# Float32 scores for the first 20 heads, maxima transposed in their own slot, and four constant matmuls at the head of ten slots

## The chip, the core and the metric

The kernel runs on one core of one Trainium2 chip. The metric is the device time of one execution in microseconds. TensorE (PE in the profile) multiplies matrices and PEld loads its weights, VectorE (DVE) reduces and combines, ScalarE (ACT) applies functions, GpSimd (POOL) works elementwise, and SyncE (SP) only issues DMAs. GpSimd and ScalarE issue DMAs too, each in the order of its own instructions.

## What is computed

Block-causal attention for 8 batches of 8 heads, and then a two-layer network with a gate on the joined heads:

```python
batch, n_heads, seq, head_dim = (8, 8, 576, 64)
scores = scale * np.matmul(q, k.transpose(0, 1, 3, 2))        # scale = 1/8
mask = block_i >= block_j                                      # blocks of 64
scores = np.where(mask, scores, -1000000000.0)
attn = np.exp(scores - np.max(scores, axis=-1, keepdims=True))
attn = attn / (np.sum(attn, axis=-1, keepdims=True) + 1e-09)
x = np.matmul(attn, v)                    # heads joined: 4608 x 512
h = x @ w_in                              # 512 x 2048
sp = np.maximum(h, 0.0) + np.log1p(np.exp(-np.abs(h)))
out = (h * erf(sp)) @ w_out               # 2048 x 512
```

q and k are scaled so that the scores are large; all arrays are float32.

## The kernel before

**Slots.** The 64 heads are worked through one per slot. In slot n the kernel computes the exponentials of head n's scores (`probs`, lines 437 to 468), the row maxima of head n+2 (`maxes`, lines 393 to 435), starts the load of head n+3 (`load_qk`, lines 377 to 391), and in every second slot multiplies two heads' exponentials with V (`pv`, lines 470 to 523). Every fourth slot normalises four heads and writes their part of x to DRAM (`normalise`, line 547). Beside that run the conversion of the network's weights (`conv`, two half weights in most early slots, lines 116 to 126; `split_w`, lines 141 to 148, from slot 9) and, from slot 10 on, steps of the network itself (`moe1`, line 267; up at line 190, gate at lines 159 to 167, down at line 199): none in slots 0 to 9 that find work, 12 steps a slot to slot 19, 28 from slot 20. What is left of the network follows after the last slot.

**Order.** Each slot is a set of lists of steps; each list has a stretch of the slot, for example 0 to 0.6, its steps are spread evenly over it, and `merge` (line 214) sorts all steps of the slot by that place. Each engine then works its own instructions in a fixed order and waits for what an instruction needs. Buffers are in rings; a step that writes a buffer waits for its last reader.

**Scores.** Head n has one buffer of `qks`, four heads deep (line 265), with four parts of 576 columns: klh, qhl, kh, qh. kh and qh are k and q rounded to float32r as a GpSimd DMA writes them; klh and qhl hold in one half of the partitions what rounding left off (`low`, lines 388 and 389, two subtractions on GpSimd, from an exact copy `st` that SP loads, two buffers deep) and in the other half the rounded values. A piece of the scores is two matmuls into one bank (lines 446 and 447): kh with qh, over 64 rows, four mask rows and one row with the negated maxima, and klh with qhl over 128 rows. ScalarE takes the exponential (line 451). There are six pieces with 1856 columns in all.

**Maxima.** Each step a, b, c, d(0), d(1) of `maxes` is one or two matmuls of rounded q and k (line 400) and VectorE reductions (line 403). Step e transposes the five columns of maxima on TensorE (line 430), ScalarE copies them (line 432) and issues the DMA that puts them as one row into the head's buffer (line 433; "qk<-mt" in the profile). The five steps of head n+2 are spread over slot n; e is put off to slot n+1, where it is alone in the stretch 0 to 0.6.

**Start.** Three heads are loaded; the mask rows come once from DRAM on GpSimd's queue and are copied to the other three buffers by DMAs on ScalarE's queue (lines 586 to 599). In slots 0 and 1 ten constant matmuls each (`warm`, line 646: a 128 x 32 array of ones, 512 columns, float16, into a bank that nothing reads) are spread over the slot.

**V.** In the first three batches (`B32`), V and the exponentials are kept in float32 and line 495 multiplies them in float32; later they are split into two float16 parts, three products each.

Of the kernel before, what the change touches and what calls it, by code (L numbers as in the profile page):

```python
# [32 lines left out]
def tile_attention_moe(ctx: ExitStack, tc: tile.TileContext, qk, v, w, maskrows, sels, out):  # L33
# [13 lines left out]
    T = 256  # L47
    GA = 8
    B32 = 3
    SH = 384  # L50
    N = B * H

# [209 lines left out]
    scaled = [False, False]  # L262
    todo = []
    NB = 4
    qks = [wpool.tile([P, 4 * S + 64], F32R, name=f"qk{i}", bufs=1) for i in range(NB)]

    def moe1(ready):

# [25 lines left out]
    with tc.tile_pool(name="apool", bufs=2) as apool, tc.tile_pool(name="spool", bufs=1) as spool, \  # L294
# [77 lines left out]

        def part(n, i):

            return qks[n % NB][:, i * S : (i + 1) * S]

        def load_qk(n):
            b, h = divmod(n, H)
            t = qks[n % NB][:, : 4 * S].rearrange("p (i n) -> p i n", n=S)
            st = apool.tile([P, S], F32, tag="st", name=f"st_{n}", bufs=2)  # L380

            def a():
                nc.gpsimd.dma_start(t[:D, 1:4, :], qk[b, h, D:].rearrange("(s d) n -> d s n", d=D))
                nc.sync.dma_start(st, qk[b, h, : 2 * D])
                nc.gpsimd.dma_start(t[D:, 0:2, :], qk[b, h, : 2 * D].rearrange("(s d) n -> d s n", d=D))

            def c():
                nc.gpsimd.tensor_tensor(out=t[:D, 0, :], in0=st[:D, :], in1=f32(t[:D, 2, :]), op=ALU.subtract)  # L388
                nc.gpsimd.tensor_tensor(out=t[D:, 1, :], in0=st[D:, :], in1=f32(t[D:, 1, :]), op=ALU.subtract)  # L389

            return a, c

        def maxes(n):

            mx, K = mxs[n % 2], D + 4
            kh, qh = part(n, 2), part(n, 3)

            def mm(dst, i, k0, w_):
                r = min(P, S - i * P)
                nc.tensor.matmul(dst[:r, :w_], lhsT=qh[:K, i * P : i * P + r], rhs=kh[:K, k0 : k0 + w_], start=True, stop=True)  # L400

            def red(col, src, r=P):
                nc.vector.tensor_reduce(out=mx[:r, col : col + 1], in_=src, axis=AX.X, op=ALU.max, negate=True)  # L403

            def a():
                s = bank(f"s01_{n}")
                mm(s, 0, 0, 256)
                mm(s[:, 256:], 1, 0, 256)
                red(0, s[:, :128])
                red(1, s[:, 256:])  # L410

            def b():
                s = bank(f"s2_{n}")
                mm(s, 2, 0, 384)
                red(2, s[:, :384])

            def c():
                s = bank(f"s3_{n}")
                mm(s, 3, 0, 512)
                red(3, s)  # L420

            def d(j):
                s = bank(f"s4_{n}_{j}")
                mm(s, 4, 288 * j, 288)
                red(5 + j, s[:64, :288], 64)

            def e():
                nc.vector.tensor_reduce(out=mx[:64, 4:5], in_=mx[:64, 5:7], axis=AX.X, op=ALU.min)
                pt = bank(f"mt{n}")
                nc.tensor.transpose(out=pt[:5, :P], in_=mx[:, :5], identity=ident)  # L430
                mt = apool.tile([5, P], F32R, tag="mt", name=f"mt_{n}")
                nc.scalar.copy(mt, pt[:5, :P])
                nc.scalar.dma_start(f32(qks[n % NB][D + 4 : D + 5, 3 * S :]).rearrange("o (i p) -> o i p", p=P), f32(mt))

            return [a, b, c, lambda: d(0), lambda: d(1), e]

        def probs(n, out):
# [4 lines left out]
            def one(j, q0, w_, o):  # L442
                kk = min(P, S - j * P)
                ks = slice(j * P, j * P + kk)
                s = bank(f"t{j}_{n}_{q0}")
                nc.tensor.matmul(s[:kk, :w_], lhsT=kh[:K, ks], rhs=qh[:K, q0 : q0 + w_], start=True, stop=False)  # L446
                nc.tensor.matmul(s[:kk, :w_], lhsT=klh[:, ks], rhs=qhl[:, q0 : q0 + w_], start=False, stop=True)  # L447
                skip = max(0, starts[j] - q0)
                part, c = offs[j]
                c += q0 + skip - starts[j]  # L450
                nc.scalar.activation(p32s[part][:kk, c : c + w_ - skip], s[:kk, skip:w_], AF.Exp, scale=SCALE)  # L451
# [132 lines left out]
        vs, prs, usbs = {}, {}, {}  # L584
        normals, ready_at, ready = {}, {}, 0
        heads = [load_qk(n) for n in range(NB - 1)]
        masks = [qks[n][D : D + 5, 2 * S : 4 * S] for n in range(NB)]
        nc.gpsimd.dma_start(masks[0], maskrows)
        for m in masks[1:]:
            nc.scalar.dma_start(f32(m), f32(masks[0]))  # L590
        heads[0][0]()
        sel = spool.tile([P, 4], F32, name="sel")
        nc.sync.dma_start(sel, sels)
# [30 lines left out]

        PRIO = {}
        WARM = 10
        LQ = 0.1
        TOF = {0: 1, 1: 1, 2: 2, 3: 2, 4: 2, 5: 2, 6: 2, 7: 2, 8: 2} | {n: 2 for n in range(11, 19)}
        SCALE_AT = {9: 0, 20: 1}
# [20 lines left out]
        for n in range(N + 3):  # L650
# [3 lines left out]
                lists += [(late("load", [load]), 0, LQ), (late("low", [low]), LQ, 1)]  # L654
            if n + 2 < N:
                *steps, rows[n + 2] = maxes(n + 2)
                lists.append((late("max", steps), 0, 1))
            if n + 1 in rows:
                lists.append((late("max", [rows.pop(n + 1)]), 0, 0.6))
            if n < N:  # L660
                prs[n] = []
                lists.append((late("prob", probs(n, prs[n])), 0, 1))
# [77 lines left out]
```

## Time and profile before

| | |
|---|---|
| median of 3 runs | 1251.46 us (1250.63 to 1252.27) |
| the profiled execution | 1253.77 us, span 1252.0 us |
| TensorE busy | 1169.7 us, 93% |
| ScalarE busy | 865.4 us, 69% |
| VectorE busy | 791.9 us, 63% |
| GpSimd busy | 515.9 us, 41% |
| DMA | 151.73 MB, mean 121 GB/s |
| granted TensorE clock, mean | 0.970 |

The profile gives times from the first instruction on. In a view of waits, a row names the engine and line that stood idle, what ended its wait, the total in us, how often, and the longest one. In the chain of work that ended last, and in the timeline, a row has start, duration, engine and line. The view of windows gives busy time by engine in stretches of the span, with the clock that TensorE was granted as a share of full speed. "t" is a bank of scores, "s" a bank of scores for the maxima, "u" one of products with V; "qk<-qk" is the load of a head. A matmul's recorded time includes its way through the array, so the pace of a stream is read from the starts of its matmuls. A matmul on float32 operands is recorded as two matmuls and two weight loads.

### The profile page before, as it was taken

What the parts mean: (1) busy time and instruction counts of PE and PEld (TensorE: products, weight loads), DVE (VectorE), ACT (ScalarE), POOL (GpSimd) and SP (SyncE); (2) the same over time, 40 slices, a digit from 0 to 9 for tenths busy, and PEclk for the clock granted to TensorE, in tenths of its full rate; (3) what the DMA queues carried; (4) which work ended last, traced back from release to release, by engine and by line L of the source; (5) the groups of instructions that cost most, each with busy time, mean ns of one, the idle gap of its engine ahead of it and who ended that gap; (6) DMA issues with size and microseconds to landing.
All of it is one profiled execution on the core that took longest, in us unless ns stands there. A gap on an engine that the chain in (4) does not pass through costs nothing.

```text
span 1252.0 us, 23446 instructions
## 1 busy us (share of the span) xinstructions
PE 1169.7 (93%) x9018; PEld 811.0 (65%) x9018; DVE 791.9 (63%) x1457; ACT 865.4 (69%) x1699; POOL 515.9 (41%) x486
## 2 busy tenths in 40 slices
PE   5788699989999999999999899999999999999896
PEld 2465466666666767767767677766777766666563
DVE  4677689787577666676657667666666644343433
ACT  1465577687676777877777677777777876666664
POOL 6455446545343444445444353545443313121211
PEclk9876799999999999999999999999999999999999
DMA  9988569744544455364454455455554121121211
GB/s 218 250 208 190 124 181 234 195 101 117 112 128 110 115 125 128 100 147 120 99 124 116 118 119 130 112 124 128 112 137 108 45 78 53 60 76 35 64 55 51
DMA packets 95741, 151.73 MB, mean 121 GB/s; under 512 B 7738, under 2 KB 44922, under 8 KB 95630
## 3 DMA queue, kind: packets, MB, share of 16 engines
q1 hardware_dynamic: 69840, 93.34, 25.7%
q0 software_dynamic: 25120, 56.66, 22.6%
q8 instruction: 71, 1.16, 0.4%
q10 hardware_dynamic: 670, 0.23, 0.2%
q14 instruction: 40, 0.33, 0.1%
HBM read 121.66 MB, written 28.31 MB: 120 GB/s over the span
## 4 chain that ended last, share of the span: by engine, by line
PE 49%; DVE 20%; ACT 18%; DMA 7%; issue 4%; POOL 1%; DVEq 0%; SPq 0%; POOLq 0%; ACTq 0%
PE m_h L190 16%; PE o L199 15%; PE u L495 5%; DVE m_r L163 4%; DVE m_r L164 4%; DVE m_r L165 3%; ACT m_r L160 3%; ACT m_r L162 3%; ACT m_r L161 3%; ACT m_r L159 3%; PE t L446 3%; PE s L400 3%; PE t L447 2%; DMA qk<-qk 2%; DMA qk<-mt 2%
## 5 line engine op out<-in xcount | busy, mean ns | idle before, releaser
L190 PE MATMUL m_h<-xh,w 128*128 128x256 f16 x2304 | 476.1, 276 | 19.5 <-DVE m_r L165 12.2
L190 PEld LDWEIGHTS <-w 128*128 128x128 f16 x3456 | 328.3, 99 | 158.1 <-issue 31.2
L199 PE MATMUL o<-w,m_gh 128*128 128x512 f16 x1152 | 334.1, 382 | 12.2 <-DVE pt L240 4.9
L167 POOL TENSOR_TENSOR m_gl<-m_r,m_gh 128x512 f16<-128x512 f32 x144 | 171.8, 1193 | 391.1 <-ACT m_gh L166 340.6
L190 PE MATMUL m_h<-xl,w 128*128 128x256 f16 x1152 | 316.8, 275 | 0.5 <-DMA xl<-x_d 0.5
L403 DVE TENSOR_REDUCE mx<-s 64x1 f32<-64x288 f32 (+4 forms) x384 | 174.5, 469 | 131.3 <-PE s L400 130.5
L163 DVE SCALAR_TENSOR_TENSOR m_r<-m_r,m_r 128x512 f32<-128x512 f32 x144 | 112.8, 783 | 197.3 <-ACT m_r L162 190.8
L199 PE MATMUL o<-w,m_gl 128*128 128x512 f16 x576 | 203.7, 384 | 0.3 <-POOL m_gl L167 0.3
L451 ACT ACTIVATE p<-t 128x288 f32<-128x288 f32 (+4 forms) x384 | 144.6, 384 | 79.4 <-PE t L447 69.1
L166 ACT CAST m_gh<-m_r 128x512 f16<-128x512 f32 x144 | 88.9, 617 | 157.2 <-DVE m_r L165 154.4
L446 PE MATMUL t<-qk 69*128 69x288 f32 (+4 forms) x384 | 168.2, 439 | 13.0 <-DMA qk<-mt 6.8
L400 PE MATMUL s<-qk 68*64 68x288 f32 (+3 forms) x384 | 150.1, 423 | 22.8 <-DMA qk<-qk 19.8
L159 ACT ACTIVATE m_r<-m_h,c,bs 128x512 f32<-128x512 f32 (+3 forms) x192 | 124.1, 666 | 44.5 <-PE m_h L190 41.4
L388 POOL TENSOR_TENSOR qk<-st,qk 64x576 fp32r<-64x576 f32 x64 | 95.9, 1499 | 127.2 <-DMA qk<-qk 124.5
L199 PEld LDWEIGHTS <-m_gh 128*128 128x128 f16 x1152 | 100.2, 98 | 67.6 <-issue 12.3
L164 DVE SCALAR_TENSOR_TENSOR m_r<-m_r 128x512 f32<-128x512 f32 x144 | 122.6, 852 | 3.3
L447 PE MATMUL t<-qk 128*128 128x288 f32 (+4 forms) x384 | 120.0, 313 | 0.0
L463 DVE TENSOR_TENSOR p<-p,p 128x832 f16<-128x832 f32 x80 | 81.7, 1022 | 58.0 <-ACT p L462 57.9
L389 POOL TENSOR_TENSOR qk<-st,qk 64x576 fp32r<-64x576 f32 x64 | 98.4, 1538 | 39.2 <-DMA qk<-qk 29.1
L161 ACT ACTIVATE m_r<-m_r,c 128x512 f32<-128x512 f32 x144 | 103.8, 721 | 2.7 <-ACT m_r L160 0.7
L162 ACT ACTIVATE m_r<-m_r,c 128x512 f32<-128x512 f32 x144 | 103.7, 720 | 2.3 <-ACT m_r L161 0.3
L160 ACT ACTIVATE m_r<-m_r,c 128x512 f32<-128x512 f32 x144 | 103.7, 720 | 1.6
(99 smaller groups left out, 1454.8 us busy)
## 6 DMA issues: line engine op xcount, KB each, us to landing
qk<-qk POOLq DMA_DIRECT2D x64, 432.0 KB, 5.0
st<-qk SPq DMA_DIRECT2D x64, 288.0 KB
qk<-qk POOLq DMA_DIRECT2D x64, 288.0 KB, 5.6
raw<-w SPq DMA_DIRECT2D x32, 512.0 KB
v<-v SPq DMA_DIRECT2D x16, 640.0 KB
x_d<-xs POOLq DMA_DIRECT2D x32, 288.0 KB, 3.3
xh<-x_d SPq DMA_DIRECT2D x36, 256.0 KB
xl<-x_d SPq DMA_DIRECT2D x36, 256.0 KB
```

The costliest lines, as they stand in the source:

```text
L159: nc.scalar.activation(r0s[:, :, lo:hi], h[:, :, lo:hi], AF.Tanh, bias=const(p1), scale=bss[b][g][:, 0:1])
L161: nc.scalar.activation(r0, r1, AF.Square, bias=const(b2), scale=a2)
L163: nc.vector.scalar_tensor_tensor(out=r0, in0=r0, scalar=c4, in1=r1, op0=ALU.add, op1=ALU.mult)
L164: nc.vector.scalar_tensor_tensor(out=r0, in0=r0, scalar=c5, in1=r0, op0=ALU.add, op1=ALU.mult)
L167: nc.gpsimd.tensor_tensor(out=gl, in0=r0, in1=gh, op=ALU.subtract)
L190: nc.tensor.matmul(h[:, k, :], lhsT=wf[:, a, sl], rhs=x[:, cc, :], start=cc == 0 and i == 0, stop=cc == NCC - 1 and i == 2)
L199: nc.tensor.matmul(o[c], lhsT=a[:, sl], rhs=wf[:, b_, :], start=u == u0 and k == 0 and not lo and b_ == 2, stop=u == u1 - 1 and k == nu - ...
L400: nc.tensor.matmul(dst[:r, :w_], lhsT=qh[:K, i * P : i * P + r], rhs=kh[:K, k0 : k0 + w_], start=True, stop=True)
L403: nc.vector.tensor_reduce(out=mx[:r, col : col + 1], in_=src, axis=AX.X, op=ALU.max, negate=True)
L446: nc.tensor.matmul(s[:kk, :w_], lhsT=kh[:K, ks], rhs=qh[:K, q0 : q0 + w_], start=True, stop=False)
L447: nc.tensor.matmul(s[:kk, :w_], lhsT=klh[:, ks], rhs=qhl[:, q0 : q0 + w_], start=False, stop=True)
L451: nc.scalar.activation(p32s[part][:kk, c : c + w_ - skip], s[:kk, skip:w_], AF.Exp, scale=SCALE)
```

## The change

For heads 0 to 19 (`N32`) the scores are one float32 matmul per piece, with exact k and q in a float32 buffer; the maxima of these heads are still taken from rounded k and q, which now lie in a buffer of their own (`lows`). These heads are loaded by two DMAs of 288 KB, one on GpSimd's queue into `lows` and one on SP's into `qks`, and have no subtractions. From head 20 on the buffers of `qks` are taken anew as float32r and `lows` holds klh and qhl; scores and subtractions are as before, rounded values come by three DMAs in place of two with the same bytes in all, and heads 20 to 23 load the mask rows again. At the start, `lows` and `qks` both get mask rows, seven DMAs on ScalarE's queue in place of three.

In slots 0 to 9 (`SOON`), the five steps of the maxima of head n+2 are spread over 0 to 0.7, step e follows at 0.9 of the same slot, and four of the constant matmuls stand at the head of the slot (0 to 0.04). Slots 0 and 1 keep their ten as well. In slot 0 the row of head 1, put off from before the loop, is still transposed in the stretch 0 to 0.6.

```diff
+    N32 = 20
...
-    qks = [wpool.tile([P, 4 * S + 64], F32R, name=f"qk{i}", bufs=1) for i in range(NB)]
+    lows = [wpool.tile([P, 2 * S], F32R, name=f"ql{i}", bufs=1) for i in range(NB)]
+    qks = [wpool.tile([P, 2 * S + 64], F32, tag="qk", name=f"q32_{i}", bufs=NB) for i in range(NB)]
...
-            return qks[n % NB][:, i * S : (i + 1) * S]
+            return (lows if i < 2 else qks)[n % NB][:, i % 2 * S : (i % 2 + 1) * S]
...
-            t = qks[n % NB][:, : 4 * S].rearrange("p (i n) -> p i n", n=S)
+            if N32 <= n < N32 + NB:
+                qks[n % NB] = wpool.tile([P, 2 * S + 64], F32R, tag="qk", name=f"qk{n}", bufs=NB)
+            lo, hi = [x[n % NB][:, : 2 * S].rearrange("p (i n) -> p i n", n=S) for x in (lows, qks)]
+            if n < N32:
+                src = qk[b, h, : 2 * D].rearrange("(s d) n -> d s n", d=D)
+
+                def whole():
+                    nc.gpsimd.dma_start(lo[:D], src)
+                    nc.sync.dma_start(hi[:D], src)
+
+                return whole, lambda: None
...
             def a():
-                nc.gpsimd.dma_start(t[:D, 1:4, :], qk[b, h, D:].rearrange("(s d) n -> d s n", d=D))
+                if n < N32 + NB:
+                    nc.gpsimd.dma_start(qks[n % NB][D : D + 5, : 2 * S], maskrows)
+                nc.gpsimd.dma_start(hi[:D], qk[b, h, : 2 * D].rearrange("(s d) n -> d s n", d=D))
+                nc.gpsimd.dma_start(lo[:D, 1, :], qk[b, h, D : 2 * D])
                 nc.sync.dma_start(st, qk[b, h, : 2 * D])
-                nc.gpsimd.dma_start(t[D:, 0:2, :], qk[b, h, : 2 * D].rearrange("(s d) n -> d s n", d=D))
+                nc.gpsimd.dma_start(lo[D:], qk[b, h, : 2 * D].rearrange("(s d) n -> d s n", d=D))
...
-            kh, qh = part(n, 2), part(n, 3)
+            kh, qh = [part(n, i) for i in ((0, 1) if n < N32 else (2, 3))]
...
-                nc.tensor.matmul(s[:kk, :w_], lhsT=kh[:K, ks], rhs=qh[:K, q0 : q0 + w_], start=True, stop=False)
-                nc.tensor.matmul(s[:kk, :w_], lhsT=klh[:, ks], rhs=qhl[:, q0 : q0 + w_], start=False, stop=True)
+                nc.tensor.matmul(s[:kk, :w_], lhsT=kh[:K, ks], rhs=qh[:K, q0 : q0 + w_], start=True, stop=n < N32)
+                if n >= N32:
+                    nc.tensor.matmul(s[:kk, :w_], lhsT=klh[:, ks], rhs=qhl[:, q0 : q0 + w_], start=False, stop=True)
...
-        masks = [qks[n][D : D + 5, 2 * S : 4 * S] for n in range(NB)]
-        nc.gpsimd.dma_start(masks[0], maskrows)
-        for m in masks[1:]:
-            nc.scalar.dma_start(f32(m), f32(masks[0]))
+        nc.gpsimd.dma_start(lows[0][D : D + 4], maskrows[:4])
+        for n in range(NB):
+            if n:
+                nc.scalar.dma_start(f32(lows[n][D : D + 4]), f32(lows[0][D : D + 4]))
+            nc.scalar.dma_start(qks[n][D : D + 5, : 2 * S], maskrows)
...
+        SOON = 10
...
                 *steps, rows[n + 2] = maxes(n + 2)
-                lists.append((late("max", steps), 0, 1))
+                lists.append((late("max", steps), 0, 0.7 if n < SOON else 1))
             if n + 1 in rows:
                 lists.append((late("max", [rows.pop(n + 1)]), 0, 0.6))
+            if n < SOON:
+                lists.append((late("max", [rows.pop(n + 2)]), 0.8, 1))
+                lists.append(([warm] * 4, 0, 0.04))
```

More of the change, by code (lines that the diff above doesn't have):

```diff
@@ L373, in part @@
         def part(n, i):
-            return qks[n % NB][:, i * S : (i + 1) * S]
+            return (lows if i < 2 else qks)[n % NB][:, i % 2 * S : (i % 2 + 1) * S]
         def load_qk(n):
             b, h = divmod(n, H)
-            t = qks[n % NB][:, : 4 * S].rearrange("p (i n) -> p i n", n=S)
+            if N32 <= n < N32 + NB:
[7 more added lines that the diff above has]
+                return whole, lambda: None
             st = apool.tile([P, S], F32, tag="st", name=f"st_{n}", bufs=2)
             def a():
-                nc.gpsimd.dma_start(t[:D, 1:4, :], qk[b, h, D:].rearrange("(s d) n -> d s n", d=D))
+                if n < N32 + NB:
+                    nc.gpsimd.dma_start(qks[n % NB][D : D + 5, : 2 * S], maskrows)
+                nc.gpsimd.dma_start(hi[:D], qk[b, h, : 2 * D].rearrange("(s d) n -> d s n", d=D))
+                nc.gpsimd.dma_start(lo[:D, 1, :], qk[b, h, D : 2 * D])
                 nc.sync.dma_start(st, qk[b, h, : 2 * D])
-                nc.gpsimd.dma_start(t[D:, 0:2, :], qk[b, h, : 2 * D].rearrange("(s d) n -> d s n", d=D))
+                nc.gpsimd.dma_start(lo[D:], qk[b, h, : 2 * D].rearrange("(s d) n -> d s n", d=D))
             def c():
-                nc.gpsimd.tensor_tensor(out=t[:D, 0, :], in0=st[:D, :], in1=f32(t[:D, 2, :]), op=ALU.subtract)
-                nc.gpsimd.tensor_tensor(out=t[D:, 1, :], in0=st[D:, :], in1=f32(t[D:, 1, :]), op=ALU.subtract)
+                nc.gpsimd.tensor_tensor(out=lo[:D, 0, :], in0=st[:D, :], in1=f32(hi[:D, 0, :]), op=ALU.subtract)
+                nc.gpsimd.tensor_tensor(out=lo[D:, 1, :], in0=st[D:, :], in1=f32(lo[D:, 1, :]), op=ALU.subtract)
             return a, c
@@ L432, in e @@
                 nc.scalar.copy(mt, pt[:5, :P])
-                nc.scalar.dma_start(f32(qks[n % NB][D + 4 : D + 5, 3 * S :]).rearrange("o (i p) -> o i p", p=P), f32(mt))
+                nc.scalar.dma_start(f32(qks[n % NB][D + 4 : D + 5, S:]).rearrange("o (i p) -> o i p", p=P), f32(mt))
             return [a, b, c, lambda: d(0), lambda: d(1), e]
```

## The prediction

> **What bounds the kernel now.** I read the windows first, cut where the stages end: the first score matmul of a slot (line 446) gives slot 0 its start at 24.75 us, slot 10 at 118.84 and slot 20 at 255.02. The columns are busy time by engine (with a count), then granted TensorE clock, DMA share and GB/s.
>
> ```profile
> core 0: us, PE busy (x) PEld busy (x) DVE busy (x) ACT busy (x) POOL busy (x), PEclk, DMA share, GB/s
> 0.00:24.75 24.75, 11.04 (x32) 5.04 (x32) 7.45 (x21) 1.54 (x2) 17.43 (x37) 1.00 1.13 228
> 24.75:118.84 94.09, 78.00 (x484) 52.12 (x484) 68.56 (x157) 53.55 (x147) 43.22 (x41) 0.78 0.92 223
> 118.84:255.02 136.18, 120.92 (x880) 81.93 (x879) 105.24 (x207) 93.18 (x216) 69.17 (x59) 0.91 0.70 177
> 255.02:1252.00 996.98, 959.72 (x7625) 671.87 (x7625) 610.68 (x1075) 717.15 (x1336) 386.13 (x350) 0.99 0.40 101
> ```
>
> Behind slot 20 TensorE is busy for 959.72 of 996.98 us at a clock of 0.99: it is the bound there, and the instructions of heads 20 and later stay what they were. The change therefore acts on the first 255 us. In the start-up nothing but loads matters. In slots 0 to 9 three things are short together: the DMA engines are 92% taken, TensorE is idle for 16.1 us, and the clock gives away 22% of 94.09 us, 20.7 us. In slots 10 to 19 TensorE is idle for 15.3 us and the clock loses 9% of 136.18 us, 12.3 us.
>
> Next, whom TensorE waits for, first between 25 and 60 us, then 60 to 100, then 100 to 160 (us in total, times, longest):
>
> ```profile
> PE s L400 <- DMA qk<-qk: 5.0, 2, 2.7
> PE t L446 <- DMA qk<-mt: 4.7, 3, 2.9
> ```
> ```profile
> PE s L400 <- DMA qk<-qk: 2.2, 2, 1.4
> PE t L446 <- DMA qk<-mt: 2.1, 2, 1.1
> ```
> ```profile
> PE m_h L190 <- DMA xh<-x_d: 7.2, 1, 7.2
> ```
>
> Of the 16.1 idle us in slots 0 to 9, 7.2 wait for a head's load and 6.8 for the row of maxima, which travels by DMA from its transpose (line 430) to the head's buffer; half of the 15.3 later ones is one wait for the first x tile. The chain of waits shows how the start hangs together (start, us, what):
>
> ```profile
> 14.47 1.41 POOL qk L389
> 15.89 0.33 SPq L384
> 16.27 0.47 SPq L326
> 16.84 8.15 DMA raw<-w
> 25.01 0.68 ACT a L120
> ...
> 26.44 3.44 DMA qk<-mt
> ```
>
> The low part on GpSimd, SP's next head load that waits for it, the v load and the weight load queued behind that on SP, ScalarE's conversion of the weights, and behind it the row of maxima.
>
> Last, the clock in shorter stretches (same columns as above):
>
> ```profile
> 71.00:85.00 14.00, 12.37 (x46) 8.23 (x47) 9.83 (x17) 8.21 (x20) 7.58 (x6) 0.51 0.78 184
> 108.00:112.00 4.00, 4.00 (x50) 3.63 (x40) 2.96 (x10) 3.06 (x9) 1.26 (x2) 1.00 0.60 165
> 112.00:126.00 14.00, 12.77 (x52) 8.02 (x50) 12.05 (x31) 8.92 (x20) 8.79 (x6) 0.51 0.61 122
> 136.00:147.00 11.00, 6.18 (x32) 4.26 (x32) 2.13 (x3) 1.91 (x3) 2.78 (x2) 0.53 0.83 156
> ```
>
> TensorE counts as busy through most of two stretches of 14 us at half clock; one of them follows on 4 us without a gap.
>
> **The change part by part.** *Float32 scores, heads 0 to 19.* Two float32r matmuls per piece (lines 446 and 447) become one in float32. First the old price, at full clock, by starts:
>
> ```profile
> 49.72 0.31 PE L446 MATMUL t<-qk 69*128 69x320 f32 x1
> 49.88 0.31 PE L447 MATMUL t<-qk 128*128 128x320 f32 x1
> 50.02 0.63 PE L400 MATMUL s<-qk 68*128 68x256 f32 x3
> ```
>
> A pair of 320 columns takes 0.30 us, 0.93 ns a column, and a head has 288+288+256+256+448+320 = 1856 columns, 1.73 us. No float32 score exists in this trace; the nearest rows are the products with V, float32 in the first three batches and float16 later:
>
> ```profile
> 303.70 3.00 PE u L495 x28
> 308.40 0.86 PE o L199 x4
> 314.37 1.67 PE us L518 x24
> ```
> ```profile
> 375.55 2.18 PE u L495 x42
> ```
>
> Both of line 495 cover 2 x 1600 columns, the two heads of a pair in the two halves of the array. In float16 with three terms that is 9600 columns in 2.18 us, 0.23 ns each, so the halves run side by side: one matmul alone takes 0.42 ns a column (four of 512 at line 199 in 0.86 us). In float32, 1600 column pairs in 3.00 us are 1.88 ns each, four times that and a little. A float32 score fills the array alone, so a head costs between 1856 x 4 x 0.42 = 3.1 us and 1856 x 1.88 = 3.5 us; I take 3.3, 1.6 more than now. If the halves did not run side by side, the low end, a head would cost 1.7 and nothing be added. Twenty heads at 1.6: 16 us in slots 0 to 9 and 16 in slots 10 to 19, on the engine nearest to being the bound.
>
> *Loads and low parts of heads 0 to 19.* The 432 and 288 KB on GpSimd's queue and 288 KB on SP's become 288 and 288 KB. The maxima read their own buffer, whose last reader is three slots back, so its load no longer waits for the probabilities of the slot before. The two subtractions go from GpSimd, and with them SP's wait for their staging buffer. What I read of it:
>
> ```profile
> qk<-qk POOLq DMA_DIRECT2D x14, 432.0 KB, 6.4
> qk<-qk POOLq DMA_DIRECT2D x13, 288.0 KB, 6.8
> ```
> ```profile
> SPq L384 <- POOL qk L389: 34.4, 8, 8.9
> ```
>
> The first two are DMA issues of 0 to 119 us (count, KB each, us to landing), the last is SP's wait from 24 to 119. By 119 us some 14 heads save 432 KB each, 6 MB of the 223 GB/s x 119 us = 26.5 MB moved: the DMA engines then need about 92 us for what takes 119, so they stop being the bound, and the 7.2 us of waits for loads go. At the start, SP issues its v and weight loads without the wait for the subtraction: the chain loses the 1.41 us at 14.47, and the first load is 288 KB in place of 720 KB on one queue. I take 5 us off the start-up; the bounds are 1 (the subtraction alone) and 8 (the whole stretch from 16.84 to 25.0 that waits for weights).
>
> *Maxima transposed in their own slot.* Their row is issued some 0.4 slot earlier, about 4 us with slots of 9.4 (94.09/10), which is more than the longest single wait for it, 2.9: the 6.8 us go. The price is a wait that the trace hardly has: the transpose stands in TensorE's order soon after its last score, and VectorE must have reduced it. Queued behind it are the next slot's scores, and ScalarE's exponentials wait for those. The nearest row is TensorE's wait for VectorE's reductions at the scores, over the first 320 us:
>
> ```profile
> PEld t L446 <- DVE mx L403: 4.8, 7, 1.3
> ```
>
> Bounds: 0, and the 1.3 of the longest, in every slot; I take 0.2 a slot, 2 us in all, which is about what these waits come to per slot now (4.8 us over some 24 slots), because VectorE keeps a quarter of this stage free.
>
> *Four constant matmuls in each of ten slots.* Each streams 512 columns in float16, 0.215 us at full clock by line 199's row: forty cost 8.6 us, 17 at half clock, and nothing where they fall into idle time.
>
> *The clock.* At full clock the work of slots 0 to 9 now lies between 52 us, summed from rows (ten heads at 1.73 for scores and 1984 columns at half of 0.93 ns, 0.9, for maxima, four pairs at 3.00 + 1.67, two normalisations at some 3.5, of which line 556 is 1.24, below), and busy time by clock, 78.0 x 0.78 = 61. I take 57, which is 61% of 94.09 us.
>
> ```profile
> 224.83 1.24 PE rt L556 x12
> ```
>
> After the change it is 57 + 16 + 8.6 = 81.6 us in fewer microseconds, above 85%. Both half-clock stretches of 14 us ended only in the long unbroken float32 products with V:
>
> ```profile
> 81.38 4.36 PE L495 MATMUL u<-p,v 128*64 128x128 f32 x22
> ```
> ```profile
> 120.95 5.48 PE L495 MATMUL u<-p,v 128*64 128x256 f32 x28 [0.52 <-ACT p L451]
> ```
>
> Float32 scores are the same kind of stream. I take the clock to 0.95 in slots 0 to 9 and 0.97 in the next ten.
>
> The page "TensorE: Matmul & The Clock Gate" of the Trainium skill (Part 1: The HAM clock gate) has the clock halve only after a window of some 3.4 us without work and rise after as long a busy one. The rows of 71 to 85 and 108 to 126 speak against that: 4.00 busy of 4.00 us and then half clock, and 12.37 of 14 us busy without a rise. By that rule four constant matmuls are too short to lift the clock, and yet it would stay full as soon as the long waits go; what that would give is the second rival.
>
> *The sum.* Start-up: -5. Slots 0 to 9: 81.6 of work, 4 of idle time (16.1 - 7.2 - 6.8 = 2, and 2 at the transposes), 4.3 lost to the clock, 89.9 against 94.1: -4.2. Slots 10 to 19: +16 of scores, -5 of the 7.2 at the first x tile, whose load stood on SP behind a head load held up by a subtraction, -8.3 of clock (12.3 to 4), -2 of other idle time filled: +0.7. Behind slot 20, one more GpSimd issue per head, 44 at 0.65 us, and four mask loads lie in GpSimd's free time (386.13 of 996.98 us busy): 0, or some 3 if a tenth of them holds something up. Together -8.5.
>
> ```profile
> L383 POOL DMA_DIRECT2D qk<-qk x64 | 41.4, 646 | 129.0 <-PE t L447 112.1 <-PE o L199 12.6 <-PE s L400 3.7
> ```
>
> ```profile
> 123.83 9.12 SPq L384 DMA_DIRECT2D st<-qk  x2
> 133.12 0.39 SPq L222 DMA_DIRECT2D xh<-x_d  x1
> ```
>
> The last two rows are those of SP on which the -5 rests. The profiled execution took 1253.77 us (span 1252.0), the median of the runs is 1251.46; 8.5 off the median is 1243.
>
> **The rivals.** *Slower: float32 at the clock of today.* If the clock follows waiting rather than streaming and stays at 0.78 and 0.91, the added 24.6 us cost 31.5 in slots 0 to 9 on top of 78.0 busy, with 4 idle 113.5 (+19.4); slots 10 to 19 get 16/0.91 - 7 = +10.6; with -5 at the start +25, 1276. It decides from the point where less than half of the lost clock comes back (there the sum is near +8, 1260). For it: 12.77 of 14 us busy at a clock of 0.51. Against: those stretches are full of short, latency-bound matmuls.
>
> *More gain: all of the lost clock returns.* If the half clock comes only of waiting, it goes with the waits for loads, maxima and x tile: the 4.3 and the 4 left in the sum go too, 1234.5; with 8 at the start, 1231.5. This is the page's rule carried through. For it: those waits were most of TensorE's idle time. Against it: the half-clock stretches with little idle time.
>
> *No change: VectorE and ScalarE set the pace.* VectorE is busy 68.56 of 94.09 and 105.24 of 136.18 us; if the removed waits come back as waits of the transposes and exponentials (the bound of 1.3 us a slot in place of 0.2, 11 us in slots 0 to 9), the gain of 8.5 is gone: 1251 to 1254.
>
> **How the numbers follow.** Forecast 0.42, more gain 0.21, no change 0.14, slower 0.23. About 0.2%, 2.5 us, is what a measurement can tell. Below 1249 lie the larger gain and nine tenths of the forecast, with a little of the no-change case: 0.62. Within: 0.12; above: 0.26. The range goes from 1229, below the larger gain, to 1260, where half of the clock comes back; beyond it lies the worse half of the slower case.
>
> **What would show it.** Right: no wait of line 446 for the row of maxima and none of line 400 for loads before 119 us; a granted clock of 0.9 or more in slots 0 to 9; a float32 score of 288 columns every 0.48 to 0.54 us; slot 0 starting near 20 us and slot 10 near 110; the stretch behind slot 20 within 3 us of 997. Wrong: a clock still under 0.85, transposes waiting for VectorE by over 1 us a slot, slots 10 to 19 longer than 142 us, or a score at half the price assumed.

## The result, and the profile after

The changed kernel takes 1258.1 us, the median of 20 runs (1249.26 to 1268.42), the kernel before 1251.57 (20 runs): a ratio of 1.0053, 95% interval 1.0033 to 1.0073 (it leaves out the run of 1268.42 as a slow one). It is slower by half a per cent; 8.5 us faster was forecast. The profiled execution of the changed kernel took 1252.59 us, 5.5 under its own median; that of the kernel before, 1253.77, lies 2.2 over its own. So the two profiles show a difference of -1.2 us where the runs show +6.5. The runs of the changed kernel say where the rest is: at a mean granted clock of 0.982 or more they take 1249 to 1254 us (one 1262.6), at 0.975 to 0.978 they take 1257 to 1268.

To set the profiles side by side I cut both at the same instruction of each slot, the exponential of the 64 rows of a head's last block, in slots 0, 9 and 20. Windows of the kernel before (length, busy time of PE, PEld, DVE, ACT and POOL with counts, clock, DMA share, GB/s):

```profile
0.00:26.32 26.32, 12.61 (x43) 6.50 (x44) 8.79 (x24) 2.85 (x7) 17.43 (x37) 1.00 1.14 234
26.32:116.19 89.87, 73.78 (x464) 48.64 (x464) 64.57 (x151) 50.12 (x139) 41.00 (x40) 0.79 0.94 227
116.19:274.39 158.20, 140.91 (x1011) 95.55 (x1010) 126.80 (x248) 110.60 (x251) 82.69 (x69) 0.92 0.66 164
274.39:1252.00 977.61, 942.39 (x7505) 660.27 (x7503) 591.78 (x1037) 701.85 (x1307) 374.83 (x341) 0.99 0.40 101
```

And of the changed kernel:

```profile
0.00:28.20 28.20, 15.25 (x45) 6.77 (x45) 10.62 (x26) 3.36 (x7) 6.36 (x28) 1.00 0.98 199
28.20:118.30 90.10, 89.74 (x505) 48.36 (x503) 58.96 (x151) 50.90 (x138) 10.00 (x14) 0.90 0.65 183
118.30:276.38 158.08, 148.14 (x1006) 93.56 (x1007) 118.15 (x245) 110.40 (x248) 50.08 (x51) 0.95 0.53 138
276.38:1250.80 974.42, 943.72 (x7508) 661.09 (x7505) 587.53 (x1038) 703.39 (x1308) 393.82 (x381) 0.99 0.39 102
```

The second row of each is the case. The stage lasts as long as before, 90.10 against 89.87 us, but it is another stage: the DMA share went from 0.94 to 0.65, GpSimd from 41 us to 10, the clock from 0.79 to 0.90, and TensorE from 73.78 us busy to 89.74 of 90.10. TensorE's waits between the two cuts are one row:

```profile
PE s L415 <- DVE mx L418: 0.3, 1, 0.3
```

The chain of waits, summed by line over this stage, before and after (the answer breaks off at the right):

```profile
by line: DMA qk<-mt 28.4%; PE u L495 21.7%; PE t L446 8.8%; DMA qk<-qk 8.2%; PE us L518 6.4%; PE s L400 5.9%; PE t L447 5.2%; ACT p L451 2.6%; ACT a L120 1.8%; issue 1.4%; PE rb L575 1.3%; PE rt L556 1.3%; ACT mt L432 1.2%; PE mt L430 0.8%;
```
```profile
by line: PE t L461 35.5%; PE u L511 14.4%; PE s L415 13.8%; PE warm L665 12.1%; DMA v<-v 6.3%; PE us L534 5.6%; PE rb L591 3.7%; PE mt L445 1.7%; DVE vm L338 1.6%; PE rt L572 1.4%; DVE mx L418 1.1%; DVE w L148 0.7%; DVE usb L593 0.7%; issue
```

Before, 28% of the chain is the way of the maxima and 8% the loads of heads. Afterwards neither is in the row, and float32 scores (line 461, "t") and constant matmuls (line 665, "warm") have taken their room. One slot of that chain, without a gap on TensorE:

```profile
41.33 0.49 PE t L461 x2
41.82 3.00 PE u L511 x28
44.82 0.43 PE s L415
45.25 0.43 PE t L461 x2
45.68 0.13 PE s L415
45.82 0.11 PE vt L340
45.93 0.57 PE t L461 x2
46.51 0.28 PE s L415
46.78 0.75 PE t L461 x2
47.53 1.67 PE us L534 x24
49.20 0.20 PE mt L445
49.41 0.54 PE t L461 x2
49.95 0.97 PE warm L665 x4
```

With the piece of 0.49 just ahead of it (at 40.66), a head's six scores take 0.49 + 0.49 + 0.43 + 0.57 + 0.75 + 0.54 = 3.27 us; four constant matmuls take 0.97.

The half clock has not gone. It stands at the two normalisations of the stage, in slots 5 and 9; the first of the two, and the full-clock stretch behind it:

```profile
72.70:86.40 13.70, 13.70 (x41) 7.10 (x42) 7.63 (x18) 5.72 (x15) 4.62 (x5) 0.50 0.55 162
...
86.40:113.60 27.20, 27.20 (x195) 16.02 (x191) 14.38 (x40) 13.20 (x38) 1.84 (x3) 1.00 0.50 133
```

TensorE is busy for all of the 13.7 us at half clock, and constant matmuls stand in them (1.39 us for three at 75.86, in the chain).

### The profile page after: what moved, and what is told of

Read it like the earlier page. It is cut to its first block, busy times and chain, and to the rows that moved or that the text cites. A ratio compares the mean times of both kernels' runs of the same rounds, so it can differ in the third digit from the quotient of the medians.

```text
span 1250.8 us, 23571 instructions
## 1 busy us (share of the span) xinstructions
PE 1196.8 (96%) x9058; PEld 809.8 (65%) x9058; DVE 775.3 (62%) x1457; ACT 868.1 (69%) x1699; POOL 460.3 (37%) x474
## 4 chain that ended last, share of the span: by engine, by line
PE 48%; DVE 21%; ACT 20%; DMA 5%; issue 4%; POOL 1%; DVEq 0%; ACTq 0%; POOLq 0%; SPq 0%
PE m_h L191 14%; PE o L200 14%; PE t L461 5%; DVE m_r L164 5%; DVE m_r L165 4%; PE u L511 4%; DVE m_r L166 4%; ACT m_r L161 4%; ACT m_r L162 4%; ACT m_r L163 3%; PE s L415 3%; ACT m_r L160 3%; ACT m_gh L167 2%; DVE p L479 2%; DMA v<-v 2%
## 5 line engine op out<-in xcount | busy, mean ns | idle before, releaser
L200 PE MATMUL o<-w,m_gh 128*128 128x512 f16 x1152 | 336.2, 384 | 10.8 <-ACT ob L243 4.4
L160 ACT ACTIVATE m_r<-m_h,c,bs 128x512 f32<-128x512 f32 (+3 forms) x192 | 124.2, 666 | 37.5 <-PE m_h L191 35.4
L461 PE MATMUL t<-qk 69*128 69x288 f32 (+4 forms) x264 | 119.9, 454 | 0.2 <-DVE mx L418 0.2
L479 DVE TENSOR_TENSOR p<-p,p 128x832 f16<-128x832 f32 x80 | 85.2, 1065 | 53.7 <-ACT p L478 53.5
L165 DVE SCALAR_TENSOR_TENSOR m_r<-m_r 128x512 f32<-128x512 f32 x144 | 114.6, 796 | 3.4
L415 PE MATMUL s<-qk 68*64 68x288 f32 (+3 forms) x264 | 108.6, 439 | 1.4 <-ACT usb L514 1.3
L166 DVE SCALAR_TENSOR_TENSOR m_r<-m_r,m_h 128x512 f32<-128x512 f32 x144 | 98.0, 680 | 4.8
L461 PE MATMUL t<-q 69*128 69x288 f32 (+3 forms) x240 | 88.7, 458 | 1.1 <-DVE mx L418 1.1
L511 PE MATMUL u<-p,v 128*64 128x320 f16 (+9 forms) x1176 | 85.9, 297 | 3.1 <-DVE p L479 3.0
```

Of the source, the lines that this page charges most:

```text
L160: nc.scalar.activation(r0s[:, :, lo:hi], h[:, :, lo:hi], AF.Tanh, bias=const(p1), scale=bss[b][g][:, 0:1])
L165: nc.vector.scalar_tensor_tensor(out=r0, in0=r0, scalar=c5, in1=r0, op0=ALU.add, op1=ALU.mult)
L166: nc.vector.scalar_tensor_tensor(out=r0, in0=r0, scalar=fin, in1=flat, op0=ALU.add, op1=ALU.mult)
L200: nc.tensor.matmul(o[c], lhsT=a[:, sl], rhs=wf[:, b_, :], start=u == u0 and k == 0 and not lo and b_ == 2, stop=u == u1 - 1 and k == nu - ...
```

## The experiments

Ratios are to the kernel before, run beside each variant on the same chip, with 95% intervals of 0.2 to 0.4% to either side. A difference between two experiments is read from two such ratios, so it is known to 4 or 5 us. The profiles are cut as above.

**Without the four constant matmuls** (no_warm)

```diff
-                lists.append(([warm] * 4, 0, 0.04))
```

> The changed kernel without the four constant matmuls of slots 0 to 9 (the ten of slots 0 and 1 stay). Two theories of why the change lost 6.5 us instead of winning 8.5. Theory A, TensorE's stream: since the waits for loads and maxima are gone, the first ten slots last as long as TensorE's work, and each microsecond added there is paid in full. Then this kernel is 6 to 9 us under the changed one, near 1250, and slots 0 to 9 take about 86 us in place of 94.5. Theory B, the clock: the half-clock stretches that stayed (72.7 to 86.4 and 113.6 to 130.7 us in the profile of the changed kernel) are what is lost, and work that keeps the array streaming helps; then it is at 1258 or above, with a lower mean clock.

1242.69 us, 0.9951 (0.9925 to 0.9977): faster than both kernels, by some 13 us than the changed one (1.0053 - 0.9951 of 1250; the two intervals leave 9 to 17). Its stage, slots 0 to 9 and 9 to 20:

```profile
28.81:109.50 80.69, 79.30 (x466) 47.17 (x465) 59.24 (x154) 52.11 (x142) 10.30 (x14) 0.86 0.73 203
109.50:266.29 156.79, 150.59 (x1006) 93.98 (x1007) 113.12 (x242) 108.30 (x247) 51.18 (x51) 0.94 0.53 139
```

Theory A holds, with more gained than its 6 to 9 us, and theory B falls: 36 matmuls lie between the first two cuts, and the stage is 9.4 us shorter without them (90.10 to 80.69), 0.26 us each. The clock is lower without them in this pair, 0.86 against 0.90, and the stage is shorter all the same. Its length times its clock, an estimate of what it needs at full clock, is 69 us against 81. The whole spans of the two profiles differ by 9.3 us.

**Twice as many** (warm8)

```diff
-                lists.append(([warm] * 4, 0, 0.04))
+                lists.append(([warm] * 8, 0, 0.04))
```

> The changed kernel with eight constant matmuls at the head of slots 0 to 9 in place of four. Theory A: each is paid in full at 0.24 us at full clock and 0.43 at half clock, so 40 more cost 10 to 17 us: 1267 to 1275. Theory B (they lift the clock if there are enough): the mean clock goes over 0.985 and the time stays at 1258 or falls. Rival D (the cost is the break in the stream, once per slot): under 5 us more, 1259 to 1263.

1273.43 us, 1.0185 (1.0149 to 1.022), some 16 more than with four.

```profile
27.89:128.27 100.38, 100.06 (x545) 52.06 (x543) 61.44 (x154) 51.21 (x137) 9.95 (x14) 0.90 0.60 166
128.27:293.47 165.20, 156.69 (x1006) 96.81 (x1007) 115.27 (x241) 110.77 (x249) 50.10 (x51) 0.90 0.49 130
```

80.69, 90.10 and 100.38 us with none, four and eight, or 69, 81 and 90 at full clock by the same estimate: each four add about the same, as theory A has it, and the clock is 0.90 with four and with eight. That the three lengths lie on so straight a line is luck in part, as the profile of n32_10 below shows. Rival D, one break in the stream per slot, falls. The stage behind is longer too, 165.20 against 158.08 us, at a clock of 0.90 against 0.95.

**The same, over the whole width of the array** (warm_wide)

```diff
+        def warm_wide():
+            nc.tensor.matmul(ps_w, lhsT=ones[:, :64].bitcast(F16), rhs=ones32[:, None, :].broadcast_to([P, 16, 32]), start=True, stop=True)
...
-                lists.append(([warm] * 4, 0, 0.04))
+                lists.append(([warm_wide] * 4, 0, 0.04))
```

> The changed kernel with its four constant matmuls a slot made 128 columns wide in the weights (the float32 ones read as float16 pairs) in place of 32: same stream of 512 columns, the whole array filled. Theory B2: the clock follows how much of the array works, and the narrow matmuls are too small to hold it; then the half-clock stretches of 13.7 and 17.1 us at the two normalisations shrink, the mean clock is over 0.985 and the time is 1246 to 1252. Theory A: they are paid like the narrow ones and change nothing else: 1255 to 1262 at a mean clock of 0.975 to 0.985.

1260.62 us, 1.0082 (1.0048 to 1.0116), mean clock 0.975 in the profile and 0.978 in the median run: theory A again, no lift. In its profile the stretch at the first normalisation is gone, and a longer one, 27 us at half clock, stands from 26 to 54.

**Early transposes and constant matmuls alone, on the kernel before** (soon_only), and **early transposes alone** (early_only)

```diff
-                lists.append((late("max", steps), 0, 1))
+                lists.append((late("max", steps), 0, 0.7 if n < SOON else 1))
...
+            if n < SOON:
+                lists.append((late("max", [rows.pop(n + 2)]), 0.8, 1))
+                lists.append(([warm] * 4, 0, 0.04))                  # soon_only alone
```

> The kernel before with the early transposes and the four constant matmuls alone, scores and loads as before. Theory A: TensorE has 16.1 us of idle time in slots 0 to 9 to take the 8.6 us, and the 6.8 us of waits for the maxima go; the waits for loads stay: 1244 to 1251. Theory B: the constant matmuls lift the clock from 0.78 to 0.9 in slots 0 to 9, a gain of 10 or more: below 1243.

> The kernel before with the early transposes alone: the steps of the maxima over 0 to 0.7 of the slot and the transpose at 0.9 of the same slot in slots 0 to 9, no constant matmuls, scores and loads as before. Theory A (TensorE's stream is paid in full, waits are what can be won): the 6.8 us of waits for rows of maxima go and nothing is added, 1241 to 1246, 1 to 5 under the kernel that has the constant matmuls as well. Rival C: with the loads of heads still late, the wait only moves from the maxima to the loads and to VectorE: 1248 to 1251.

1246.11 us, 0.9975 (0.9949 to 1.0002), and 1247.09, 0.9987 (0.9965 to 1.0008). Neither is told apart from the kernel before, nor one from the other. So the early transposes bring nothing that can be told apart as long as the loads are late, as rival C had it, though its 1248 to 1251 was missed by 1 us. The same 40 constant matmuls that cost 13 us in the changed kernel cost nothing here, where TensorE has room. They do raise the clock: the median run has a mean of 0.977 with them, and 0.970 without them and in the kernel before.

**Float32 scores and new loads alone** (n32_only)

```diff
-        SOON = 10
+        SOON = 0
```

> The changed kernel with SOON = 0: float32 scores and the new loads stay, the maxima are transposed in the next slot as before, and there are no constant matmuls in slots 2 to 9. Theory A: 8.6 us of work goes, some of the 6.8 us of waits for the rows of maxima return: 1251 to 1256, and above the kernel without constant matmuls by 2 to 5. Theory B: more half clock than in the changed kernel, 1260 or more.

1249.62 us, 1.0007 (0.9979 to 1.0035): no change against the kernel before, and 7 us over the kernel that has the early transposes as well (0.9951). That is theory A's direction; its size, 2 to 5, and its 1251 to 1256 were missed. On these loads the early transposes are worth some 7 us (2 to 12 by the intervals); on the old ones nothing can be told.

**Float32 for ten heads** (n32_10, and no_warm_n10 without the constant matmuls)

```diff
-    N32 = 20
+    N32 = 10
```

> The changed kernel with float32 scores for heads 0 to 9 only (N32 = 10). Theory A: slots 10 to 19 get 16 us of TensorE work back, of which 5 to 8 go to the loads and subtractions that return: 1247 to 1253. Theory B: what these heads cost is set by the clock, which is at 0.95 in these slots with float32; with fewer streaming matmuls it falls, and nothing is won: 1256 to 1262.

> The changed kernel without the constant matmuls of slots 0 to 9 and with float32 scores for heads 0 to 9 only. Theory A: 16 us of TensorE work leave slots 10 to 19, the loads and subtractions that return there cost part of it; with the constant matmuls in place the same step gave 3.5, so 1236 to 1241. Rival E: from slot 10 on the float32 heads pay for themselves, since they free the queues that carry the first x tile: 1242 to 1247.

1254.64 us, 1.0040 (1.0012 to 1.0068), and 1241.37, 0.9927 (0.9897 to 0.9956). The second is the lowest ratio of all. Against twenty heads that is 1.6 us in the one pair and 3 in the other, less than can be told apart. Each lies between the ranges of its two theories and decides neither. The profile of no_warm_n10 from slot 9 to 20:

```profile
110.81:259.22 148.41, 136.33 (x1017) 93.15 (x1019) 123.50 (x241) 107.72 (x245) 78.17 (x76) 0.95 0.64 170
```

TensorE is busy for 136.33 us here and for 150.59 with float32 to head 19: the float32 scores of ten heads cost 14 us of work, near the 16 of the forecast. The stage is 8 us shorter (148.41 against 156.79), the loads and subtractions that come back taking the rest; between the runs it is the 3 us.

Up to slot 9, n32_10 gives TensorE the work of the changed kernel, 505 matmuls between the cuts in both. Its profile:

```profile
28.96:113.02 84.06, 83.66 (x505) 45.58 (x503) 62.81 (x151) 50.51 (x138) 24.62 (x29) 0.97 0.73 204
```

84.06 us at a clock of 0.97, where the changed kernel took 90.10 at 0.90. At full clock both come to 81 or 82 us; the half-clock stretch at the normalisation of slot 5 is not there. So the clock of a single profile is not fixed by TensorE's instructions, and 6 us of a stage can hang on it.

**Mask rows straight from DRAM** (no_warm_masks), and **staging loads of heads 20 and 21 held back** (late_st), both without the constant matmuls

```diff
-        nc.gpsimd.dma_start(lows[0][D : D + 4], maskrows[:4])
         for n in range(NB):
-            if n:
-                nc.scalar.dma_start(f32(lows[n][D : D + 4]), f32(lows[0][D : D + 4]))
+            nc.gpsimd.dma_start(lows[n][D : D + 4], maskrows[:4])
```
```diff
+                if n in (N32, N32 + 1):
+                    nc.vector.tensor_copy(st[:1, :1], mxs[n % 2][:1, 3:4])
                 nc.sync.dma_start(st, qk[b, h, : 2 * D])
```

> The changed kernel without the constant matmuls of slots 0 to 9, and with the mask rows of the rounded buffers loaded from DRAM on GpSimd's queue, four small DMAs, in place of one load and three copies on ScalarE's queue. In the changed kernel TensorE waits 4.6 us for such a copy at 10 to 15 us, 8.9 us after its source landed. Theory A: the wait goes and all behind it moves up by 3 to 5 us: 1237 to 1240. Rival F: the first weights land at 25.5 us whatever is done, and ScalarE and VectorE start with them: 1242 to 1244.

> The changed kernel without the constant matmuls of slots 0 to 9, and with the staging loads of heads 20 and 21 held back: a VectorE copy of one element of the maxima into each stands ahead of its DMA. In the changed kernel both are issued at 4.9 us, in the middle of the start-up, 576 KB of the some 3.2 MB of head loads issued in the first 11 us. If the start-up was not shortened because freed DMA time is filled by loads of later heads, 576 KB at 204 GB/s are 2.9 us: slot 0 starts 2 to 3 us earlier and the time is 1239 to 1241. Rival: the start hangs on the mask copies and on the first weights behind v, not on the amount: no change, 1242 to 1244.

1247.32 us, 0.9985 (0.9957 to 1.0013), and 1240.81, 0.9939 (0.9915 to 0.9964), against 0.9951 without either. The start-up of the changed kernel shows what they were after: SP issues the staging loads of heads 20 and 21 at 4.89 us, and the v and weight loads behind them. The kernel's text has these loads in slots 17 and 18; nothing uses their buffers before, and the planner, the program that sets each engine's order, has moved them up.

```profile
4.89 1.67 SPq L399 DMA_DIRECT2D st<-qk  x2
11.87 0.33 SPq L328 DMA_DIRECT2D v<-v  x1
14.88 11.69 SPq L114 DMA_DIRECT2D raw<-w  x3
```

So by 11 us eleven loads of 288 KB are issued, 3168 KB, against 2736 KB (432, 288 and 288 for each of three heads, the third staging load still waiting) in the kernel before: less per head, and more heads. With the mask rows from DRAM the first load, now behind four small ones on GpSimd's queue, landed at 13.74 us, against 9.43 in no_warm; with the staging loads held back the first weights were there at 21.87 us, against 26.14, and the first scores were no earlier (26.03 against 25.86):

```profile
13.74 1.99 PE L415 MATMUL s<-ql 68*128 68x256 f32 x6 [13.74 <-DMA ql<-qk]
```
```profile
21.65 4.45 PE L667 MATMUL warm<-ones 128*32 128x512 f16 x10
21.87 0.67 ACT L121 ACTIVATE a<-raw 128x512 f32<-128x512 f32 x1 [3.70 <-DMA raw<-w]
26.03 1.51 PE L463 MATMUL t<-q 69*128 69x288 f32 x4
```

In front of the first score stand ten of the constant matmuls of slots 0 and 1, 4.45 us. Taking one of the waits away leaves the next, as both rivals had it. Neither time is told apart from 0.9951: the first is above both of its forecasts, and that the second, 1240.81, lies in the range for an earlier start is luck, for the start was not earlier.

**One constant matmul in slots 0 and 1 in place of ten** (n10_warm1; no constants later, ten float32 heads)

```diff
-        WARM = 10
+        WARM = 1
```

> The changed kernel without the constant matmuls of slots 0 to 9, float32 scores for heads 0 to 9 only, and one constant matmul in place of ten in each of slots 0 and 1. Theory A: in slots 0 and 1 TensorE waits for loads anyway, so 18 fewer cost or win little, and up to 4 us where they stand in the stream: 1237 to 1242. Theory B: without them the clock is at half speed when the first scores come, and the time is 1244 or more.

1244.87 us, 0.9971 (0.9943 to 0.9999), above the 0.9927 with ten by 5 us, at the limit of what can be told apart; theory B's number. The start shows why nothing is won:

```profile
23.89 2.29 PE L461 MATMUL t<-q 69*128 69x288 f32 x4 [4.22 <-DMA q<-mt]
```

TensorE waits for the row of maxima in place of working on constants, and the first two scores take 2.29 us; in the changed kernel they take 1.24. The granted clock is recorded as 1.00 in both, so the records do not show a half clock so early, but the pace does.

**A quarter of the stream: one float32r matmul per score** (one_r); **the same issued four times over** (one_r_x4); **one_r with the constant matmuls** (one_r_warm). The first two have no constant matmuls in slots 2 to 9 beyond what is left of slot 1's; in all three, mask rows and maxima go into the rounded buffer, by lines that are left out here.

```diff
             klh, qhl, kh, qh = [part(n, i) for i in range(4)]
+            if n < N32:
+                kh, qh = klh, qhl
...
+                for _ in range(4 if n < N32 else 1):                   # one_r_x4 alone, around the matmul
```

> The changed kernel without the constant matmuls of slots 0 to 9, and with the scores of heads 0 to 19 from one float32r matmul of the rounded k and q in place of the float32 one (the part that rounding leaves off is left out; mask row and maxima go into the rounded buffers, by two DMAs). A head's scores then stream 1856 columns once, some 1.1 us with weight loads in place of 3.3. Theory A: TensorE's stream sets slots 0 to 9 and most of slots 10 to 19, so a good part of the 44 us that go is won until VectorE is next (63 of 85 us busy in slots 0 to 9): 1215 to 1228. Rival G: ScalarE, VectorE and the clock hold the slots nearly as long: 1234 to 1242.

> The kernel with one float32r matmul per piece of heads 0 to 19 (the rounded parts alone, no constant matmuls in slots 2 to 9), with each of these matmuls issued four times over with the same operands, so that a head streams 4 x 1856 columns as in float32, about 3.3 us; loads and waits as in that kernel, which took 1254. Theory B2, a long stream of real operands holds the clock: the 13.7 us stretches at half clock in slots 0 to 9 fall from four to two, and the time falls to 1243 to 1251 though 44 us of work are added. Theory A, work on TensorE is paid in full: 1275 or more. If the time stays within 1252 to 1258, stream and clock cancel.

> The kernel with one float32r matmul per piece of heads 0 to 19 and four constant matmuls at the head of slots 0 to 9, as the changed kernel has them. TensorE has idle time again here. Theory A2 (the price of a constant matmul is the room on TensorE): they cost little, 1253 to 1259, and the clock in slots 0 to 9 stays at 0.7 to 0.75. Theory B2 (any stream holds the clock): clock above 0.8 there, and 1244 to 1250. Theory D (they cost their 0.3 us whatever stands around them): 1264 to 1270.

1254.32 us, 1.0045 (1.0017 to 1.0074); 1271.45, 1.0174 (1.0134 to 1.0215); 1247.17, 0.9987 (0.9955 to 1.0019). Slots 0 to 9 and 9 to 20 of each in turn:

```profile
31.43:115.00 83.57, 72.41 (x404) 42.63 (x403) 56.67 (x147) 49.54 (x137) 14.67 (x21) 0.70 0.86 218
115.00:271.27 156.27, 134.77 (x944) 86.11 (x945) 120.16 (x247) 109.05 (x249) 53.84 (x46) 0.90 0.43 123
```
```profile
32.24:129.73 97.49, 90.44 (x572) 68.88 (x570) 59.23 (x153) 51.15 (x140) 15.74 (x21) 0.75 0.73 184
129.73:291.87 162.14, 155.47 (x1144) 112.38 (x1147) 118.33 (x242) 109.42 (x248) 47.82 (x46) 0.92 0.41 119
```
```profile
31.77:119.37 87.60, 73.14 (x445) 40.96 (x445) 57.30 (x148) 48.97 (x137) 14.02 (x21) 0.81 0.86 206
119.37:265.98 146.61, 130.12 (x944) 83.74 (x945) 117.26 (x247) 108.50 (x249) 49.88 (x46) 0.92 0.43 132
```

The first is a miss for both of its forecasts: with some 44 us less to stream (the estimate of its expectation) the kernel is 12 us slower than with float32 (1.0045 against 0.9951), the first stage is 83.57 against 80.69 us, and the clock is at 0.70 there against 0.86. The runs say the same, a mean clock of 0.960 in the median run against 0.979. These kernels have waits for loads and maxima back, since their maxima and scores share a buffer, so the clock is not the only difference; one_r_x4 adds the stream alone. It pays 16 us for it, part of the stream going into TensorE's idle time, and its clock is 0.75, 0.964 in the median run: theory B2, that any long stream of real operands holds the clock, falls here, and theory A's 1275 is missed by 4 us. At about the same amount of stream per head the float32 kernel ran at 0.86 in the same slots. And the constants turn round: here they raise the clock from 0.70 to 0.81 (0.960 to 0.967 in the median run) and the runs are 7 us shorter (0.9987 against 1.0045), in the range of theory B2 this time, though in the profiles the gain stands in slots 9 to 20.

**What the runs point to** (n10_late_st: no constants in slots 2 to 9, ten float32 heads, staging loads of heads 10 and 11 held back)

> What the experiments point to: no constant matmuls in slots 2 to 9, float32 scores for heads 0 to 9 only, and the staging loads of heads 10 and 11 held back behind the first maxima. If the gains of the two steps add (1241.4 and some 2 us), 1237 to 1241, a ratio to the kernel before of 0.990 to 0.993; if the staging loads matter only with 20 heads, 1241 to 1244.

1244.89 us, 0.9974 (0.9940 to 1.0008), just above both ranges: the two steps do not add. The lowest ratio stays the one without the staging change, 0.9927; the 0.9939 of late_st and the 0.9951 of no_warm are not told apart from it.

## Why the prediction was wrong

Cut as the prediction cut, at the first score of slots 0, 10 and 20, the profile of the changed kernel reads:

```profile
25.39:126.12 100.73, 95.19 (x524) 51.82 (x524) 68.94 (x164) 58.17 (x153) 14.03 (x18) 0.87 0.60 171
126.12:263.48 137.36, 132.60 (x903) 83.05 (x902) 98.04 (x202) 93.92 (x216) 41.90 (x44) 0.97 0.56 145
263.48:1250.80 987.32, 956.62 (x7604) 669.83 (x7602) 599.97 (x1071) 714.42 (x1330) 397.96 (x385) 0.99 0.39 102
```

Start-up, slots 0 to 9, slots 10 to 19 and the rest moved by +0.6, +6.6, +1.2 and -9.7 us; forecast were -5, -4.2, +0.7 and 0. Cut at the exponentials, as above, they are +1.9, +0.2, -0.1 and -3.2. The sum, -1.2, is the same. The stages differ because the planner has put the pieces of a slot's scores elsewhere in TensorE's order: head 20's first score stood 19.4 us ahead of its last exponential and now stands 12.9 ahead.

**Work and waits of slots 0 to 9 were right.** Of the 100.73 us, 5.5 are idle (4 were allowed) and 13.1 go to a clock of 0.87; 82 remain as work at full clock, and 81.6 were forecast. A float32 head was put at 3.3 us and takes 3.27. The waits for loads and maxima went, as the prediction said: 14.0 us before, none after. Most of the idle time is one wait of a kind that the prediction named, in slot 9, where the transpose stands behind VectorE's splitting of weights:

```profile
PE mt L445 <- DVE mx L443: 4.5, 1, 4.5
```

**The step that failed is the clock: 0.95 forecast in slots 0 to 9, 0.87 measured.** That is 13.1 us lost in place of 4.3, and 8.8 of the 10.8 us by which this stage missed. The prediction had seen half-clock stretches end in the float32 products with V, and took float32 scores for "the same kind of stream". Here they were not. In the stretch of 72.70 to 86.40 float32 scores (line 461) pass at half clock, and the clock comes back, at 86.4, in the products with V (line 511), as before the change:

```profile
78.53 2.93 PE L461 MATMUL t<-q 69*128 69x448 f32 x4
81.90 1.16 PE L461 MATMUL t<-q 69*128 69x288 f32 x2
83.18 1.16 PE L461 MATMUL t<-q 69*128 69x288 f32 x2
84.27 1.12 PE L511 MATMUL u<-p,v 128*64 128x256 f32 x4
84.75 3.59 PE L511 MATMUL u<-p,v 128*64 128x256 f32 x26
```

The second stretch of this profile and the two long ones of no_warm end in line 511 too; the long one of warm_wide ends at 53.6 us among scores, so this is no rule. What ends a stretch, no run here tells.

The Trainium skill, page "TensorE: Matmul & The Clock Gate", section "Part 1: The HAM clock gate", has the clock rise after some 3.4 us of activity; the row of 72.7 to 86.4 is 13.70 us busy of 13.70 at a clock of 0.50, so the trace does not agree, unless activity is something other than the busy time of the profile.

**Over the runs it is the same step.** The kernel before loses some 37.5 us to the clock (3.0% at its mean of 0.970). The forecast gave back 20.7 - 4.3 in slots 0 to 9 and 12.3 - 4 in the next ten, 24.7 in all, which would be a mean clock of 0.99. The median of the 20 runs is 0.98, with some 25 us lost: 13 came back, by this estimate. The one run at 0.989 took 1249.26 us. The slower rival was to decide where less than half of the lost clock returns, near 1260, and the 1258.1 fits that, though not its clock of 0.78.

**The start-up failed too: -5 forecast, +0.6 measured.** The first score comes at 25.39 us, where 24.75 was before and 20 was named. The step reckoned with less data per head. The planner filled the room with loads of more heads, and TensorE has a wait for the copied mask rows of the second head that the sum did not have:

```profile
PE s L415 <- DMA ql<-ql: 4.6, 1, 4.6
```

Behind it, constant matmuls stand ahead of the first score. Held-back loads, direct masks and fewer constants each moved one of these and gained nothing that could be told apart. Removing all at once was not tried.

**Slots 10 to 19 were right in sum and in clock:** +1.2 us against +0.7, and the 0.97 that was forecast.

**Behind slot 20** the work is unchanged; 6.5 of the -9.7 are the moved cut. Start-up and three stages make -1.2 us in the profiles; from there to the +6.5 of the medians lie the 5.5 and 2.2 us by which the two profiled executions stand under and over their medians. What lengthens the other runs of the changed kernel was not profiled; their lower mean clock points to more half clock.

**The constant matmuls** were counted at 8.6 us of work, and the gain was to come from the clock in spite of them. They cost 9.4 us in the stage and 13 (9 to 17) between the runs, and the clock did not come for them: the median run has 0.98 with them and 0.979 without. Without them the kernel is at 0.9951 of the kernel before, 6 us faster, and the rest of the change is worth having.

**When a filler pays.** Time multiplied by mean clock, medians over the runs, is an estimate of what a kernel needs at full clock. The constants add 14 us to it in the changed kernel and 15 in n32_10 (each against the same kernel without them), and 4 or 5 in soon_only and one_r_warm, where TensorE has idle time. The mean clock rises by 0.002 at most in the first two and by 0.007 in the others, which is 9 us of 1250. So they help or cost nothing where TensorE has idle time, and are paid where it has none; four cases show this, no mechanism.

**What stays open.** Why float32 scores keep a higher clock than about the same stream in float32r (the float32r kernels also wait more), what ends a half-clock stretch, and why it stays away in one execution (n32_10) and not in another of the same work.

## What to carry to other kernels

When a change takes waits away and adds work on the engine that waited, add the work up and compare it with the stage: here 81 us of work filled a 90 us stage at the clock it got, so every further microsecond, also of work meant to keep the engine warm, was paid in full. Test such fillers alone and doubled, and do not count on a clock that one kind of matmul brought for another kind. And a planner that is given less to load in the first slots may load further ahead: less data per head did not shorten the start-up here.

## What was not expected of the hardware

Half-clock stretches of 13.7 and 17.1 us stand at the normalisations in most profiles with float32 scores, with TensorE busy through all of the first one of the changed kernel; in n32_10 the one of slot 5 is missing. Four float32r matmuls of one piece ran at a clock of 0.75 in slots 0 to 9 where a float32 matmul of about the same stream ran at 0.86. And runs of one kernel spread with their mean clock: the changed kernel from 1249 us at 0.989 to 1265 at 0.978, so a single profile can stand 5 us off the median, and 11 in n10_late_st (1233.64 against 1244.89).
